# Local attention in two pieces of 1024 positions instead of three of 684, and the gate products of one pair moved back

## The chip, the cores and the metric

The kernel runs on one core of a Trainium2 chip. The core has four engines that compute and a queue of transfers. TensorE (PE) multiplies matrices and writes the results to PSUM, a small memory of eight banks. ScalarE (ACT) evaluates functions and copies. VectorE (DVE) adds and multiplies elementwise. GpSimd (POOL) does some elementwise work out of the way. SyncE (SP) issues nearly all DMA transfers. Each engine executes its own instructions in their written order, and waits on semaphores for the others.

The metric is device microseconds from one launch, the median of several runs. Lower is better.

## The reference

The input x has 2048 rows and 1024 columns. Two attention blocks read it, and a gate for each row mixes their results. Cut to what matters:

```python
g = sigmoid((x * gate_w).sum(-1, keepdims=True))
# A: linear attention, 32 heads of 32 columns
pq, pk = phi(q), phi(k)                 # phi(t) = (t + 1 if t > 0 else exp(t)) + 1e-6
kv, z  = pk^T v, pk.sum(positions)      # summed over all 2048 positions
a = (pq kv) / (pq z + 1e-6) @ A_wo
# B: each position looks back at 8 positions, 2 apart (itself, -2, ..., -14)
logits = (q . k[pos - 2*w]) * 32 ** -0.5      # w = 0..7; before position 0: masked
b = softmax(logits) v @ B_wo
out = g * a + (1 - g) * b
```

All inputs and the output are bfloat16.

## The kernel before

**Rows.** Block B only ever looks at positions of the same parity. So x is split by parity, p = 0 (even) and p = 1 (odd), with 1024 rows each, and within a parity the window is 8 consecutive rows. x is loaded transposed, in 16 tiles of 128 rows. A *pair* is two tiles 512 rows apart; pairs 0 to 3 are even rows and pairs 4 to 7 odd rows. SP issues the loads in order of pairs (`x_loads`).

**Products.** Every projection is done by `Group` with a scheme of seven products in place of eight: each of `m1` to `m7` is four matmuls of 512 columns (eight in the output stage), into a PSUM bank X or Y of the group. Between products that add onto the same bank, ScalarE copies the bank away (`save`: M1s after `m1`, U2s after `m6`, U4s after `m5`), and DVE adds a saved copy to what is in the other bank (`acc`, line 234). So `m6`, then the copy U2s, then `m5`, then the copy U4s, then `m3` are a chain on bank X. `run` writes out the order on TensorE. With g the new group and p the one before it is

```python
g.m1, g.m2, p.m3, g.m6, p.m4, g.m7, g.m5
```

so that a group is finished (`m3`, `m4`) while the next is under way. The groups are: values of B (`vb_group`, rows), keys and queries of B (`k_group`, `q_group`, columns of 4 heads by 32 for 1024 rows: slice nn and parity p), keys and values of A (`ka_group`, `va_group`), queries of A, and the output products. When an A key group finishes a row tile, it has ScalarE evaluate `exp` on it at once (`eA`, line 520).

**Side work.** After each product `side` lets one step of other work in. Generators wait in `queue`; each yields two numbers, how many products later it may go on, and how many products the shared PSUM buffer `s` (four banks, one buffer, used by attention, by kv products and by A outputs alike) counts as taken. One such generator is `attn`, queued for each of 8 combinations of nn and p two products after the queries' last product. In what follows such a combination is a round.

**Attention before.** The 1024 positions of a parity are cut into 18 blocks of 57, taken in couples j = 0 to 8, one block for each half of the partitions (b = 0, 1). Blocks hold 1026 positions, so the key and query buffers are 2050 columns wide with two zeroed columns, and the buffers V_d and OB_d in memory have SPAN = 1026 rows, of which the last two of V_d are filled with zeros. A block of 57 queries needs 64 keys: its own positions and 7 before. Columns of nn cover two chunks ch of heads. A piece t (0, 1, 2) covers 3 couples of both chunks:

- `scores(t)`: 48 matmuls of 57 columns on quarter tiles of the array (line 672), one ScalarE exp over 4 x 342 columns (678), one DVE product with the mask of zeros and ones (680).
- `pv(t)`: 48 matmuls of 57 columns with the values `vw` (690) and 8 of 342 columns that sum the weights over the keys (696); ScalarE's logarithm and exp for the reciprocal of the sums (702, 704), DVE's copy nB of the weighted values (703), DVE's product oB (706; two buffers), and a store to OB_d (707).

The order of a round is scores(0), scores(1), pv(0), scores(2), pv(1), pv(2), with at least three products between.

**Gates.** `gate(t)` is eight matmuls of one column for a tile (line 442), into one bank `gps`. `xsums(pair)` are four DVE sums of a pair's x; the last writes over half of the tile's data that the gate reads. In the beginning gates stand between groups of B values: `gates(3)` within vb_group(2), `gates(4)` behind it, `gates(5)` behind vb_group(3), `gates(6, 7)` behind vb_group(4).

Of the kernel before, what the change touches and what calls it, by code (L numbers as in the profile page):

```python
# [8 lines left out]
ACT = mybir.ActivationFunctionType  # L9
ALU = mybir.AluOpType  # L10
# [4 lines left out]
P = 128  # L15
QB = 57
NPAIR = 9
TW = 6 * QB
SPAN = 3 * TW
EPS = 1e-6  # L20
RATE_R = 0.8
OA_DELAY = 5
# [5 lines left out]
def kernel(  # L28
# [27 lines left out]

    consts = ctx.enter_context(tc.tile_pool(name="consts", bufs=1))
    dram = ctx.enter_context(tc.tile_pool(name="dram", bufs=1, space=bass.MemoryType.DRAM))
    V_d = [dram.tile([SPAN, D], BF16, name=f"V_d{p}") for p in range(2)]
    OB_d = [dram.tile([8, P, SPAN], BF16, name=f"OB_d{p}") for p in range(2)]  # L60
    OA_d = [[dram.tile([512, D], BF16, name=f"OA_d{p}{i}") for i in range(2)] for p in range(2)]

    chainp = ctx.enter_context(tc.tile_pool(name="chainp", bufs=5))
# [135 lines left out]

    maskp = consts.tile([P, 2, 6, QB], BF16, name="maskp")
    nc.gpsimd.memset(maskp[:, :, 0, :], 0.0)
    for w in range(8):
        for base in (7 - w, 71 - w):
            nc.gpsimd.affine_select(out=maskp[:, 0, 0, :], in_=maskp[:, 0, 0, :], compare_op=ALU.not_equal,
                                    fill=1.0, base=base, pattern=[[1, QB]], channel_multiplier=-1)
        nc.gpsimd.affine_select(out=maskp[0:64, 1, 0, :], in_=maskp[0:64, 1, 0, :], compare_op=ALU.not_equal,
                                fill=1.0, base=-w, pattern=[[1, QB]], channel_multiplier=-1)
    nc.gpsimd.tensor_copy(out=maskp[64:P, 1, 0, :], in_=maskp[64:P, 0, 0, :])  # L210
    for e in range(1, 6):
        nc.gpsimd.tensor_copy(out=maskp[:, 0, e, :], in_=maskp[:, 0, 0, :])
        nc.gpsimd.tensor_copy(out=maskp[:, 1, e, :], in_=maskp[:, 1 if e == 3 else 0, 0, :])
    ones = consts.tile([P, 32], BF16, name="ones")
    nc.gpsimd.memset(ones[:], 1.0)
    for p in range(2):
        nc.gpsimd.dma_start(out=V_d[p][1024:SPAN, :].rearrange("r (a e) -> (r a) e", e=P), in_=warm[0:16, 0:P])
    bd = consts.tile([P, 4, 33], F32, name="bd")
    nc.gpsimd.memset(bd[:], 0.0)
    for i in range(4):  # L220
# [125 lines left out]
    def step(force=False):  # L346
        seen = set()
        for entry in list(queue):
            if entry[4] in seen:
                continue  # L350
            seen.add(entry[4])
            if not force and (entry[0] > state["now"] or state["free"] > state["now"]):
                continue
            state["free"] = state["now"] + entry[3]
            try:
                delay, entry[3] = next(entry[1])
                entry[0] = state["now"] + delay
                state["steps"] += 1
                return True
            except StopIteration:  # L360
                queue.remove(entry)
                return step(force)
        return False
# [176 lines left out]
    def va_group(w, pair):  # L540
        vs = v_tiles("vA")

        def kv():
# [18 lines left out]
            if last:  # L562
                nc.vector.tensor_tensor(out=KVz[:].rearrange("p c (g e) -> p c g e", g=4),
                                        in0=KVacc[:, :, None, :].broadcast_to([P, 8, 4, 33]),
                                        in1=bd[:, None, :, :].broadcast_to([P, 8, 4, 33]), op=ALU.mult)
            yield 2, 2

        def done(i):
# [84 lines left out]
            f()  # L653


    def q_of(t, j, b):
        return TW * t + 2 * QB * j + QB * b

    def attn(nn, p, kT, qT, vw):

        def scores(t):
            s = side_ps("s")
            for ch in range(2):
                for j in range(3):
                    e = (3 * ch + j) * QB
                    for b in range(2):
                        q0 = q_of(t, j, b)
                        k0 = max(0, q0 - 7)  # L670
                        for g in range(4):
                            nc.tensor.matmul(s[64 * b:64 * b + 64, g, e:e + QB],  # L672
                                             lhsT=kT[32 * g:32 * g + 32, 1024 * ch + k0:1024 * ch + k0 + 64],
                                             rhs=qT[32 * g:32 * g + 32, 1024 * ch + q0:1024 * ch + q0 + QB],
                                             start=True, stop=True)
            PT = ptp.tile([P, 4, TW], BF16, name="PT", tag="PT")
            with tc.high_priority():
                nc.scalar.activation(out=PT[:], in_=s[:, :, 0:TW], func=ACT.Exp, scale=SCALE)  # L678
            m = maskp[:, 0 if t else 1, :, :].rearrange("p i q -> p (i q)")
            nc.vector.tensor_tensor(out=PT[:], in0=PT[:], in1=m[:, None, :].broadcast_to([P, 4, TW]), op=ALU.mult)  # L680
            return PT

        def pv(t, PT):
            o = side_ps("o")
            for e in range(6):
                ch, j = divmod(e, 3)
                for g in range(4):
                    for b in range(2):
                        rows = slice(64 * b, 64 * b + 64)
                        nc.tensor.matmul(o[32 * g:32 * g + 32, 2 * b, QB * e:QB * e + QB],  # L690
                                         lhsT=vw[rows, 3 * t + j, 4 * ch + g, :],
                                         rhs=PT[rows, g, QB * e:QB * e + QB], start=True, stop=True)
            for g in range(4):
                for b in range(2):
                    rows = slice(64 * b, 64 * b + 64)
                    nc.tensor.matmul(o[32 * g:32 * g + 32, 2 * b + 1, 0:TW], lhsT=ones[rows, :], rhs=PT[rows, g, :],
                                     start=True, stop=True)
            nB = ofp.tile([P, 2, TW], F32, name="nB", tag="nB", bufs=1)
            rB = ofp.tile([P, 2, TW], F32, name="rB", tag="rB", bufs=1)
            oB = ofp.tile([P, 6, 2, QB], BF16, name="oB", tag="oB", bufs=2)  # L700
            with tc.high_priority():
                nc.scalar.activation(out=rB[:], in_=o[:, 1:4:2, 0:TW], func=ACT.Ln)  # L702
                nc.vector.tensor_copy(out=nB[:], in_=o[:, 0:4:2, 0:TW])  # L703
            nc.scalar.activation(out=rB[:], in_=rB[:], func=ACT.Exp, scale=-1.0)
            num, r = (ap.rearrange("p b (e q) -> p e b q", e=6) for ap in (nB[:], rB[:]))
            nc.vector.tensor_tensor(out=oB[:], in0=num, in1=r, op=ALU.mult)
            nc.sync.dma_start(out=OB_d[p][2 * nn:2 * nn + 2, :, TW * t:TW * t + TW].rearrange("c p q -> p c q"),
                              in_=oB[:].rearrange("p (c j) b q -> p c (j b q)", c=2))

        last = None  # L710
        yield 0, 2
        for t in range(4):
            if t < 3:
                PT = scores(t)
                yield (1, 3) if last else (3, 3)
            if last:
                pv(*last)
                yield 1, 3
            last = (t, PT)

    def load_v(nn, p):
        vw = vwp.tile([P, NPAIR, 8, 32], BF16, name="vw", tag="vw")
        for b, j, n in ((0, 0, 1), (0, 1, 8), (1, 0, 9)):
            k0 = max(0, q_of(0, j, b) - 7)
            src = cols_of(V_d[p][k0:k0 + 64, :], nn)
            src = bass.AP(src.tensor, src.offset, [src.ap[0], [2 * QB * D, n], src.ap[-1]])
            nc.sync.dma_start(out=vw[64 * b:64 * b + 64, j:j + n, :, :].rearrange("p n h e -> p n (h e)"), in_=src)
        return vw
# [1 line left out]
    its = {}  # L730

    def k_group(w, nn, p):
        kT = kqp.tile([P, 2050], BF16, name="kT", tag="kq")
        nc.gpsimd.memset(kT[:, 2048:2050], 0.0)
        its[nn, p] = kT
        return Group(col_ops(w, p), lambda i, j, ps, add: acc(kT[:, 1024 * j + 512 * i:1024 * j + 512 * i + 512], ps, add))

    def q_group(w, nn, p):
        qT = kqp.tile([P, 2050], BF16, name="qT", tag="kq")
        nc.gpsimd.memset(qT[:, 2048:2050], 0.0)  # L740
        vw = load_v(nn, p)

        def done(i):
            if i == 1:
                add_side(2, attn(nn, p, its[nn, p], qT, vw), p, "attn")
        return Group(col_ops(w, p), lambda i, j, ps, add: acc(qT[:, 1024 * j + 512 * i:1024 * j + 512 * i + 512], ps, add), done)


    Wo = {}
# [117 lines left out]
    defer(2, xsums(3) + xsums(0))  # L867
    run(lambda: vb_group(2), 0)
    x_loads(6, 7)
    gates(4)  # L870
    defer(1, xsums(4) + xsums(1))
    run(lambda: vb_group(3), 0)
    load_k(0, 13)()
    load_q(0, 20)()
    gates(5)
    defer(2, xsums(5))
    run(lambda: vb_group(4), 0)
    gates(6, 7)
# [101 lines left out]
```

## Time and profile before

| | |
|---|---|
| runs | 463.18, 463.40, 464.05 us; median 463.4 us |
| profiled execution | 462.85 us, of which the span of instructions is 461.1 us |
| TensorE | 450.9 us busy (98%), 5137 matmuls |
| ScalarE | 241.6 us busy (52%) |
| DVE | 286.1 us busy (62%) |
| GpSimd | 56.6 us busy (12%) |
| DMA | 51.65 MB, 112 GB/s over the span |
| score matmuls (line 672) | 1152 of 57 columns, 66.8 to 287.2 us |
| value matmuls (lines 690, 696) | 1152 of 57 and 192 of 342 columns, 73.2 to 298.8 us |

A timeline line gives the start, the length, the engine, the line of the kernel, the operation, what it writes and reads, and the shape. A line with x4 merges four instructions in a row. Matmuls are pipelined: the length of one (379 ns at 512 columns) is longer than the distance to the next, so the distance of starts is the cost. A bracket at the end of a line names the idle time before it and what ended it.

### The profile page before, as it was taken

How to read it: one execution, taken by the hardware profiler on the slowest of the kernel's cores; microseconds unless marked ns; L12 is line 12 of the kernel's file. 1: busy time of each engine (PE TensorE's matmuls, PEld its weight loads, DVE VectorE, ACT ScalarE, POOL GpSimd, SP SyncE). 2: the span in 40 equal slices, each digit the busy share in tenths (PEclk: the TensorE clock that was granted, in tenths of full speed). 3: DMA queues.
4: the chain of work that ended last, by engine and by line, in shares of the span. 5: the costliest groups of instructions: out<-in, count | busy, mean ns of one | idle time of the engine just before them, and what ended most of it. 6: DMA issues, size and time to landing. Idle time of an engine off the chain costs nothing. (4 is left out here: it accounts for less than half of the span.)

```text
span 461.1 us, 11964 instructions
## 1 busy us (share of the span) xinstructions
PE 450.9 (98%) x5137; PEld 217.7 (47%) x5137; DVE 286.1 (62%) x458; ACT 241.6 (52%) x367; POOL 56.6 (12%) x130
## 2 busy tenths in 40 slices
PE   8989999999999999999999999999999999999997
PEld 5445444444444444444444444445554444444444
DVE  0547668769848577486684856579876973164312
ACT  1233447568568386584855848536676545222221
POOL 8000000000000000000000000006676313000000
PEclk9999999999999999999999999999999999999999
DMA  8999811590211702106021066464239872699211
GB/s 180 187 221 246 275 41 64 147 256 19 57 28 33 157 21 64 22 20 159 18 71 28 17 146 181 112 188 103 68 77 205 177 171 81 118 189 174 68 47 46
DMA packets 117941, 51.65 MB, mean 112 GB/s; under 512 B 77696, under 2 KB 115840, under 8 KB 117888
## 3 DMA queue, kind: packets, MB, share of 16 engines
q1 hardware_dynamic: 117520, 50.62, 47.1%
q8 instruction: 40, 0.66, 0.6%
q10 hardware_dynamic: 272, 0.26, 0.2%
q0 software_dynamic: 96, 0.01, 0.1%
q14 instruction: 13, 0.11, 0.1%
HBM read 25.69 MB, written 16.79 MB: 92 GB/s over the span
## 5 line engine op out<-in xcount | busy, mean ns | idle before, releaser
L252 PEld LDWEIGHTS <-xT 128*128 128x128 bf16 (+1 forms) x352 | 32.6, 98 | 37.6 <-issue 0.6
L252 PE MATMUL X<-T,SS 128*128 128x512 f16 x176 | 45.2, 379 | 0.0
L635 PE MATMUL Q<-xT,WS 128*128 128x512 bf16 x192 | 43.9, 379 | 0.5 <-DVE vA L234 0.5
L261 ACT COPY U4s<-X 128x512 f32<-128x512 f32 x40 | 23.2, 581 | 37.3 <-PE X L252 37.2
L252 PEld LDWEIGHTS <-WS 128*128 128x128 bf16 (+1 forms) x288 | 27.1, 98 | 32.9 <-issue 2.5
L678 ACT ACTIVATE PT<-s 128x1368 bf16<-128x1368 f32 x24 | 31.5, 1314 | 19.9 <-PE s L672 19.9
L252 PE MATMUL Y<-W,xT 128*128 128x512 bf16 (+1 forms) x152 | 39.1, 380 | 0.0
L252 PEld LDWEIGHTS <-SS 128*128 128x128 f16 x264 | 24.4, 98 | 27.8
L252 PE MATMUL Y<-xT,WS 128*128 128x512 bf16 (+1 forms) x144 | 37.0, 379 | 0.2 <-DVE qT L234 0.2
L252 PE MATMUL X<-SS,TS 128*128 128x512 f16 x144 | 36.9, 379 | 0.1
L680 DVE TENSOR_TENSOR PT<-PT,maskp 128x1368 bf16<-128x1368 bf16 x24 | 20.8, 867 | 20.8 <-ACT PT L678 20.8
L252 PEld LDWEIGHTS <-TS 128*128 128x128 f16 x216 | 20.5, 98 | 25.2 <-issue 1.8
L261 ACT COPY M1s<-X 128x512 f32<-128x512 f32 x40 | 23.3, 583 | 11.8 <-PE X L252 11.7
L261 ACT COPY U2s<-X 128x512 f32<-128x512 f32 x40 | 23.3, 582 | 10.4 <-PE X L252 10.4
L635 PEld LDWEIGHTS <-WS 128*128 128x128 bf16 x192 | 18.2, 98 | 20.6 <-issue 0.8
L252 PEld LDWEIGHTS <-oT 128*128 128x128 bf16 (+1 forms) x176 | 17.1, 98 | 21.8 <-DMA oT<-OA_d 1.5
L703 DVE COPY nB<-o 128x684 f32<-128x684 f32 x24 | 20.8, 867 | 6.3 <-ACT rB L702 6.0
L603 POOL TENSOR_TENSOR obA<-ofv,rec 128x512 bf16<-128x512 f32 x22 | 24.0, 1109 | 0.9
L640 ACT ACTIVATE eq<-Q 128x512 bf16<-128x512 f32 x24 | 14.3, 598 | 18.4 <-PE Q L635 17.3
L252 PE MATMUL X<-T,oS 128*128 128x512 f16 x96 | 22.7, 379 | 0.0
L252 PE MATMUL X<-W,SS 128*128 128x512 bf16 x88 | 22.7, 380 | 0.0
L252 PE MATMUL X<-W,xT 128*128 128x512 bf16 x88 | 22.6, 380 | 0.0
(137 smaller groups left out, 759.6 us busy)
## 6 DMA issues: line engine op xcount, KB each, us to landing
OB_d<-oB SPq DMA_DIRECT2D x24, 171.0 KB, 2.9
V_d<-va SPq DMA_DIRECT2D x16, 256.0 KB, 3.0
WS<-in_B_wqkv_dram SPq DMA_DIRECT2D x16, 256.0 KB, 4.2
W<-in_A_wqkv_dram SPq DMA_DIRECT2D x8, 512.0 KB, 7.0
OA_d<-obA SPq DMA_DIRECT2D x16, 256.0 KB, 2.4
out_dram<-osb SPq DMA_DIRECT2D x30, 128.0 KB, 2.0
oT<-OB_d SPq DMA_DIRECT2D x12, 256.0 KB, 4.8
vw<-V_d SPq DMA_DIRECT2D x8, 288.0 KB, 4.7
```

Of the source, the lines that this page charges most:

```text
L252: nc.tensor.matmul(ps[:], lhsT=lhsT, rhs=rhs, start=start and kc == 0, stop=kc == self.nk - 1, skip_group_check=True)
L261: nc.scalar.copy(out=s[:], in_=ps[:])
L603: nc.gpsimd.tensor_tensor(out=ob[:, k:k + 2], in0=of[:, k:k + 2, :, 0:32], in1=rec[:, k:k + 2].broadcast_to([P, 2, 8, 32]), op=ALU.mult)
L635: nc.tensor.matmul(ps[:], lhsT=w.W[:, kc, j * P:j * P + P], rhs=xT[p][:, kc, i, :], start=kc == 0, stop=kc == 7, skip_group_check=True)
L640: nc.scalar.activation(out=es[i][:, j, :], in_=ps[:], func=ACT.Exp)
L678: nc.scalar.activation(out=PT[:], in_=s[:, :, 0:TW], func=ACT.Exp, scale=SCALE)
L680: nc.vector.tensor_tensor(out=PT[:], in0=PT[:], in1=m[:, None, :].broadcast_to([P, 4, TW]), op=ALU.mult)
L703: nc.vector.tensor_copy(out=nB[:], in_=o[:, 0:4:2, 0:TW])
```

## The change

- The pieces of attention become the two chunks of heads. A piece covers 1024 positions of one chunk: 72 score matmuls, an exp and a mask product over 4 x 512 columns, 72 value matmuls and 8 sums of 512 columns, and chains of 1024 columns behind them. The order of a round is scores(0), scores(1), pv(0), pv(1). Score pieces are set at least four products apart, value pieces three.
- The last couple of blocks has 56 positions instead of 57, so that 16 x 57 + 2 x 56 = 1024 positions fit exactly. The zeroed columns and the memsets for them go; the zero rows of V_d and their two DMAs go. The last block reads 64 keys that begin at 960, and the mask is built anew for a width of 512 (32 selections instead of 24).
- oB has one buffer of 1024 columns instead of two of 684, is written by two DVE products (the couples of 57 and the last), and one store per chunk goes to contiguous rows of 2 KB.
- The values are loaded by four DMAs instead of three for a round.
- A outputs (kind "oa") are taken from the queue only when KVz is written.
- `gates(4)` moves behind vb_group(3), next to `gates(5)`.

```diff
-        def scores(t):
+        def scores(ch):
             s = side_ps("s")
...
+            for j in range(NPAIR):
+                for b in range(2):
+                    q0, n, k0 = block(j, b)
+                    for g in range(4):
+                        nc.tensor.matmul(s[64 * b:64 * b + 64, g, QB * j:QB * j + n],
+                                         lhsT=kT[32 * g:32 * g + 32, ch, k0:k0 + 64],
+                                         rhs=qT[32 * g:32 * g + 32, ch, q0:q0 + n], start=True, stop=True)
+            PT = ptp.tile([P, 4, 512], BF16, name="PT", tag="PT")
             with tc.high_priority():
-                nc.scalar.activation(out=PT[:], in_=s[:, :, 0:TW], func=ACT.Exp, scale=SCALE)
...
+                nc.scalar.activation(out=PT[:], in_=s[:], func=ACT.Exp, scale=SCALE)
+            nc.vector.tensor_tensor(out=PT[:], in0=PT[:], in1=maskp[:, None, :].broadcast_to([P, 4, 512]), op=ALU.mult)
...
-            oB = ofp.tile([P, 6, 2, QB], BF16, name="oB", tag="oB", bufs=2)
+            oB = ofp.tile([P, 1024], BF16, name="oB", tag="oB", bufs=1)
...
-        for t in range(4):
-            if t < 3:
-                PT = scores(t)
-                yield (1, 3) if last else (3, 3)
-            if last:
-                pv(*last)
-                yield 1, 3
-            last = (t, PT)
+        yield 0, 4
+        PT = [scores(0)]
+        yield 1, 4
+        PT.append(scores(1))
+        for ch in range(2):
+            yield 1, 3
+            pv(ch, PT[ch])
+        yield 1, 3
...
-    gates(4)
     defer(1, xsums(4) + xsums(1))
     run(lambda: vb_group(3), 0)
     load_k(0, 13)()
     load_q(0, 20)()
-    gates(5)
+    gates(4, 5)
```

## The prediction

> **What bounds the kernel now.** I read the page first: its busy times, then the waits and the timeline of TensorE, then the queues of ScalarE (ACT) and VectorE (DVE) in one attention round. The page:
>
> ```profile
> PE 450.9 (98%) x5137; PEld 217.7 (47%) x5137; DVE 286.1 (62%) x458; ACT 241.6 (52%) x367; POOL 56.6 (12%) x130
> ...
> PEclk9999999999999999999999999999999999999999
> ```
>
> TensorE has matmuls in flight 98% of the span, at an undiminished clock. So an edit is worth what it does to TensorE's issue: matmuls taken out, or stops of TensorE taken out or put in. Busy time hides short stops (a matmul of 512 columns is shown as 379 ns and issues every 216), so I take starts from the timeline. One attention round, TensorE:
>
> ```profile
> 191.88 1.03 PE L252 MATMUL Y<-xT,WS 128*128 128x512 bf16 x4
> 192.84 0.57 PE L672 MATMUL s<-qT,kT 32*64 32x57 bf16 x48
> 193.34 1.04 PE L252 MATMUL X<-W,SS 128*128 128x512 bf16 x4
> 194.21 1.03 PE L252 MATMUL X<-SS,TS 128*128 128x512 f16 x4
> 195.07 1.03 PE L252 MATMUL Y<-T,xT 128*128 128x512 f16 x4
> 196.03 0.55 PE L690 MATMUL o<-PT,vw 64*32 64x57 bf16 x48
> 196.39 0.37 PE L696 MATMUL o<-PT,ones 64*32 64x342 bf16 x8
> 196.69 1.04 PE L252 MATMUL Y<-xT,WS 128*128 128x512 f16 x4
> 197.57 1.03 PE L252 MATMUL X<-SS,TS 128*128 128x512 f16 x4
> 198.43 1.03 PE L252 MATMUL X<-W,xT 128*128 128x512 bf16 x4
> 199.50 0.56 PE L672 MATMUL s<-qT,kT 32*64 32x57 bf16 x48
> ```
>
> Here a product of four matmuls takes 0.864 us from start to start. A score piece (s) set between two adds 193.34-191.88-0.864 = 0.596; a value piece (o) adds 196.69-195.07-0.864 = 0.756. The last line starts 0.11 late (198.43+0.96 = 199.39): a wait for the DVE copy nB. There are eight rounds of three score and three value pieces.
>
> The one early stop, and ScalarE in the same round:
>
> ```profile
> 27.00 1.03 PE L252 MATMUL X<-T,SS 128*128 128x512 f16 x4
> 28.45 0.35 PE L442 MATMUL gps<-gw,xT 128*128 128x1 bf16 x8 [0.43 <-DMA xT<-in_A_x_dram]
> 29.91 0.35 PE L442 MATMUL gps<-gw,xT 128*128 128x1 bf16 x8 [1.11 <-DMA xT<-in_A_x_dram]
> 30.12 1.02 PE L252 MATMUL X<-W,xT 128*128 128x512 bf16 x4
> ```
>
> ```profile
> 193.47 1.31 ACT L678 ACTIVATE PT<-s 128x1368 bf16<-128x1368 f32 x1 [0.81 <-PE s L672]
> 194.68 0.58 ACT L232 CAST tA<-X 128x512 bf16<-128x512 f32 x1
> 195.29 1.06 ACT L520 ACTIVATE eA<-tA 128x1024 bf16<-128x1024 bf16 x1
> 196.25 0.57 ACT L261 COPY U2s<-X 128x512 f32<-128x512 f32 x1
> ```
>
> The copy U2s takes bank X away after its sixth product (m6, at 194.21); the fifth (m5, at 197.57) adds onto the same bank and waits for that copy. It ends at 196.82, 0.75 us before m5.
>
> **The change, part by part.**
>
> 1. *The gates of pair 4.* From 27.00 to 30.12 are 3.12 us; the product itself is 0.86, sixteen gate matmuls 0.40 (22.74 to 23.14 elsewhere in that timeline). So 1.86 us are wait. Moved one group back, both pairs' gates stand near 33.9, and the last x tile of pair 5 landed at 32.65 (issued by SP at 28.37). Nothing is late there: the 0.8 us of the 32 gates is the old work, and pair 4's in-place DVE difference, which overwrites what the gate reads, comes in the queue only after the next group's first product. **-1.86** (if pair 5 came 1.3 us later, the gain would begin to shrink).
>
> 2. *Pieces.* Matmul count and columns hardly change: 144 score and 144 value matmuls a round before and after; the sums over keys are 24x342 columns before and 16x512 after. What goes is entering and leaving. A score piece of 48 has 47 starts in about 0.57-0.21 = 0.36 us, 7.7 ns each; the other 0.23 of 0.596 is fixed. Of a value piece, 48 starts take 0.35 (196.03 to 196.39 rounded), 7.4 ns each. After: score 0.596+24x0.0077 = 0.78; value 0.756+24x0.0074+170 columns x 0.42 ns (0.864/4/512) = 1.005. Old: 24x(0.596+0.756) = 32.4. New: 16x1.785 = 28.6. **-3.85.** The Trainium skill, TensorEngine Tiling (Array Packing), Key Properties, says that changing the tiling mode drains TensorE. It states no price; counted by matmuls and columns alone this part would be 0, by the row's fixed share it is 3.85. I take the row.
>
> 3. *Waits of the third pieces.* The 0.11 above occurs in six rounds, and in the second round are 0.63 (same copy, behind a large weight sum on DVE) and 0.05. There is no third piece any more: **-1.4.** The eighth round's last value piece, now among the A queries at 298.43, is pulled forward, and with it goes a late vA addition: Q starts at 302.35 instead of 299.97+1.73, **-0.65.**
>
> 4. *The new wait.* The first score piece now needs both halves of qT, so the last DVE addition of that group. In all eight rounds that addition ends 0.07 us before the piece starts (188.88+0.69 against 189.64). Handing over costs about 0.05, as where nB (ends 199.45) releases the piece at 199.50. Cost 0, by 0.02; bound 0 to 0.1 each.
>    The second score piece is put four products after the first, not three, since the first exp is longer. So it now comes *after* the group's third product (m3), and ScalarE's built order becomes tA cast, eA exp, the long exp of scores, then U2s. Count from the start of m3. TensorE reaches m5 after m3 with the turn into tiling (0.86+0.09), the score piece (0.55+0.14), m6, m4 and m7 (2.59): 4.23. ScalarE: m3 ends at 0.65+0.38 = 1.03; cast 0.04+0.58; eA 0.03+1.06, to 2.74; then the exp of 2048 columns. Rows: 684 columns 0.74 (a logarithm), 1368 columns 1.31, so 0.85 ns a column and 1.89 for 2048, overlapping its predecessor by 0.1 (194.68 starts before 193.47+1.31): 4.53; U2s 0.57-0.1: 5.02; handover 0.05. m5 can start at 5.07, **0.84 late**, where it had 0.75 to spare. This occurs where a group of A keys is being finished in front: seven of eight rounds, since the first has no eA. **+5.9** (bounds 0.6 and 1.0 a round).
>    Behind the blocked m5 stands the value piece, behind U2s the second eA exp, the U4s copy and the logarithm of the sums; they shift with it and are not paid twice.
>    The rule that speaks against this change is in the Trainium skill, TensorE: Matmul & The Clock Gate, the table at its head: ScalarE's queue is strictly first in, first out. The row agrees in kind: X was ready at 195.24, the U2s copy began at 196.25 behind eA. Were it free to pass, this term would be 0 and the sum -7.5. I take the queue.
>
> 5. *Second value piece.* It needs the o buffer free: the logarithm (1.03 by the same slope) and DVE's nB of 1024 columns (rows: 0.69 at 512, 0.87 at 684, so 1.23). On DVE ahead of nB stand the second mask product (0.42 at 512, 0.87 at 1368, so 1.23) and about 2.4 us: kT's addition and key functions or weight sums. Following that queue, nB ends about level with the piece's turn: 0 to 0.04 in ordinary rounds, about 0.5 in the second, with its 1.2 us weight sums. **+0.7**, bounds 0 and 2.4 (0.3 a round); the lower since only the second round has long sums.
>
> 6. *oB, now one buffer.* The second piece's quotient waits for the first store. The store is issued some 2.9 us before DVE would write again; DVE's next addition (vA) is not needed until 0.9 later. Landing takes:
>
> ```profile
> OB_d<-oB SPq DMA_DIRECT2D x24, 171.0 KB, 2.9
> V_d<-va SPq DMA_DIRECT2D x16, 256.0 KB, 3.0
> ```
>
>    The new store is 256 KB in rows of 2 KB, like V_d's: 3.0. Cost 0 by about 0.85 us.
>
> 7. *Rest.* At the end TensorE stops 1.16 for the transposed OA tiles (350.64 against 348.62+0.86) and 0.49 at 339.17. The A outputs now come four matmuls (0.86) earlier beside the queries, ScalarE serves a query exp ahead of each (+0.3 on the POOL-and-DMA chain): **-0.5**, bounds -1.2 and +0.3. The longer mask building on POOL (32 selections instead of 24), done by about 15 us, has until 68; the fourth vw load adds about 0.5 us of SP and value pieces come 9 us after it; the removed zero fills and memsets were waited for by nobody on the path. All 0.
>
> Sum: -1.86-3.85-1.4-0.65+5.9+0.7-0.5 = **-1.7** against the profiled execution's 462.85 (span 461.1 and 1.8 around it). The runs' median is 0.55 above that; I carry the difference over: **461.8 us.**
>
> **Rivals.**
> *A. The exp does not block (5 in 100).* If the second exp ran early enough or m5's wait had slack, the sum is -7.5: 455.9. For it: ACT is busy only 52%. Against: the walk above, in which every duration is a row.
> *B. The store of oB decides (15 in 100), slower.* Landing was 2.1 to 4.1 for OB_d and up to 7.8 for V_d in the busy start. Beyond 3.85 us from issue, each excess stops DVE's vA addition, and with it the fourth product of that group on TensorE. At an average of 4.5 in eight rounds: +5.2, so 467.0. It turns the result slower from about 4.2 on. Against: during attention the DMA engines are only 32% busy.
> *C. The terms cancel (17 in 100).* Block at its upper bound (+1.1), second value pieces at 0.1 a round: 463.3, not to be told from before.
> *D. The forecast (63 in 100)*: 461.8, own range 460.2 to 462.6.
>
> **How the numbers follow.** Below 0.2% (0.9 us) this kernel's measurement cannot tell a difference, so faster is below 462.5. Faster: D but for a few in 100, and A, 0.65. Same: C, 0.17. Slower: B and the tail of C, 0.18. The range takes D with its bounds and C, leaves out A and the far half of B: 459.8 to 464.3.
>
> **What would show it.** Gate matmuls near 34 with no DMA wait; score pieces about 0.78 and value pieces about 1.0; a wait of m5 on the U2s copy of 0.8 us seven times, with U2s directly behind the exp of 2048 columns; no wait longer than 0.1 at a first score piece; a DVE wait on the oB store under 0.9 us. The prediction is wrong if m5 does not wait (A), or a fourth product waits on DVE after each second value piece (B).

## The result, and the profile after

The changed kernel takes 461.28 us (median of 4, 461.04 to 461.71), the kernel before 463.29 beside it (462.98 to 464.05): ratio 0.9955, 95% interval 0.9938 to 0.9972. The profiled execution took 461.23 with a span of 459.5, against 462.85 and 461.1. TensorE's last matmul starts at 455.37 instead of 457.35. So 1.98 us have gone from TensorE's row of starts, and that row is what has to be explained.

The page of the changed kernel. TensorE has 64 matmuls fewer, and the rows of OB_d move in less time (last column: median us from issue to landing). The loads of before come first; its stores, shown in the prediction, took 2.9:

```profile
oT<-OB_d SPq DMA_DIRECT2D x12, 256.0 KB, 4.8
```

```profile
PE 447.7 (97%) x5073; PEld 217.7 (47%) x5073; DVE 282.3 (61%) x450; ACT 235.9 (51%) x343; POOL 59.4 (13%) x117
...
OB_d<-oB SPq DMA_DIRECT2D x16, 256.0 KB, 2.1
oT<-OB_d SPq DMA_DIRECT2D x12, 256.0 KB, 4.0
```

What TensorE waits for (total us, times, longest), first before, then after:

```profile
PE gps L442 <- DMA xT<-in_A_x_dram: 1.5, 2, 1.1
...
PE X L252 <- DMA oT<-OA_d: 1.0, 1, 1.0
...
PE s L672 <- DVE nB L703: 0.6, 1, 0.6
PE Q L635 <- DVE vA L234: 0.5, 1, 0.5
PE oA L592 <- ACT ofv L594: 0.3, 1, 0.3
PE Y L252 <- DVE qT L234: 0.2, 1, 0.2
```

```profile
PE X L252 <- ACT U2s L261: 4.5, 7, 0.7
...
PE o L689 <- DVE nB L701: 0.6, 1, 0.6
PE o L689 <- issue: 0.5, 1, 0.5
```

The six waits shown of the first list are gone: for pair 4's x tiles, the OA tiles, nB (ahead of a third score piece), vA, ofv and qT. At the head of the second stands a new one: a product into bank X that waits for the copy U2s, seven times. TensorE's timeline shows the places:

```profile
33.31 1.03 PE L252 MATMUL X<-T,SS 128*128 128x512 f16 x4
34.17 0.94 PE L444 MATMUL gps<-gw,xT 128*128 128x1 bf16 x32
34.97 1.02 PE L252 MATMUL X<-W,xT 128*128 128x512 bf16 x4
...
161.76 1.03 PE L252 MATMUL X<-W,SS 128*128 128x512 bf16 x4
162.72 0.77 PE L673 MATMUL s<-qT,kT 32*64 32x57 bf16 x72
163.42 1.04 PE L252 MATMUL X<-SS,TS 128*128 128x512 f16 x4
...
166.84 1.02 PE L252 MATMUL X<-SS,TS 128*128 128x512 f16 x4 [0.66 <-ACT U2s L261]
...
289.17 0.65 PE L689 MATMUL o<-PT,vw 64*32 64x57 bf16 x61
290.32 0.23 PE L689 MATMUL o<-PT,vw 64*32 64x57 bf16 x11 [0.51 <-issue]
...
347.60 1.03 PE L252 MATMUL X<-SS,TS 128*128 128x512 f16 x4
348.66 1.90 PE L252 MATMUL X<-W,oT 128*128 128x512 bf16 x8
```

The 32 gate matmuls follow their product after 0.86 us, with no wait. In the round, m3 starts at 161.76 and m5 at 166.84: 5.08 us, where the prediction counted 5.07. ScalarE in the same stretch:

```profile
162.88 0.59 ACT L232 CAST tA<-X 128x512 bf16<-128x512 f32 x1 [0.74 <-PE X L252]
163.50 1.06 ACT L522 ACTIVATE eA<-tA 128x1024 bf16<-128x1024 bf16 x1
164.46 1.86 ACT L678 ACTIVATE PT<-s 128x2048 bf16<-128x2048 f32 x1
166.22 0.58 ACT L261 COPY U2s<-X 128x512 f32<-128x512 f32 x1
```

U2s, which m5 needs, stands behind the key exp and the exp of 2048 columns. Bank X had been ready since 164.46 (m6's start at 163.42 and 1.04), and the copy began at 166.22. At 289 one value piece is cut into 61 and 11 matmuls by a stop that no semaphore explains; nothing in the prediction spoke of it.

At the end, TensorE goes from its last product of A queries to the first output product. Before, this cost 2.02 us from start to start; in the changed kernel, by the last two lines above, 1.06:

```profile
348.62 1.03 PE L252 MATMUL X<-SS,TS 128*128 128x512 f16 x4
350.64 1.68 PE L252 MATMUL X<-W,oT 128*128 128x512 bf16 x7 [0.99 <-DMA oT<-OA_d]
```

Taken from start to start in the two traces:

| step | forecast, us | measured, us |
|---|---|---|
| gates of pair 4 | -1.86 | -1.86 |
| entering and leaving 16 fewer pieces | -3.85 | -3.36 |
| waits at third pieces | -1.4 | -1.38 |
| late vA ahead of Q | -0.65 | -0.65 |
| two waits in round 2 (0.38 for qT, 0.23 for bank X) gone | not foreseen | -0.6 |
| m5 behind U2s | +5.9 | +5.69 |
| second value piece, waiting for nB | +0.7 | +0.86 |
| stop inside the last value piece | not foreseen | +0.65 |
| A outputs (0.48 to 0) and first output product (1.16 to 0.20) | -0.5 | -1.44 |
| first score piece; one oB buffer | 0 | 0 |
| start of the program (first product of a group at 23.41 instead of 23.14) | 0 | +0.27 |
| many differences of at most some hundredths | 0 | -0.16 |
| sum | -1.7 | -1.98 |

The start is scatter: in the thirteen profiled executions of this case the first product of a group starts at 23.13 to 23.58, whatever the edit. The rows from the fewer pieces to the stop in the last value piece come to +1.2. So the bigger pieces by themselves make TensorE's row longer, and the end, which gains 1.44, pays for them.

### The profile page after: what moved, and what is told of

The parts are those of the page before. It is cut to its first block, busy times and chain, and to the rows that moved or that the text cites. A ratio compares the mean times of both kernels' runs of the same rounds, so it can differ in the third digit from the quotient of the medians.

```text
span 459.5 us, 11765 instructions
## 1 busy us (share of the span) xinstructions
PE 447.7 (97%) x5073; PEld 217.7 (47%) x5073; DVE 282.3 (61%) x450; ACT 235.9 (51%) x343; POOL 59.4 (13%) x117
## 4 chain that ended last, share of the span: by engine, by line
PE 90%; ACT 6%; DMA 1%; SPq 1%; issue 0%; DVE 0%; ACTq 0%; DVEq 0%
PE X L252 41%; PE Y L252 28%; PE Q L638 9%; PE K L497 3%; ACT PT L678 3%; PE o L689 2%; ACT eA L522 2%; PE oA L595 2%; DMA xT<-in_A_x_dram 1%; PE s L673 1%; PE kps L556 1%; ACT tA L232 1%; PE o L694 1%; PE Y L287 1%; ACT U2s L261 1%; PE gps L444 1%
## 5 line engine op out<-in xcount | busy, mean ns | idle before, releaser
L252 PEld LDWEIGHTS <-WS 128*128 128x128 bf16 (+1 forms) x288 | 28.1, 98 | 33.6
L463 POOL MEMSET vA<- 128x32 bf16 x16 | 3.9, 249 | 269.9 <-DVE eA L525 145.0
L678 ACT ACTIVATE PT<-s 128x2048 bf16<-128x2048 f32 x16 | 29.9, 1869 | 15.1 <-PE s L673 15.0
L679 DVE TENSOR_TENSOR PT<-PT,maskp 128x2048 bf16<-128x2048 bf16 x16 | 19.6, 1224 | 22.1 <-ACT PT L678 22.1
L606 POOL TENSOR_TENSOR obA<-ofv,rec 128x512 bf16<-128x512 f32 x22 | 25.7, 1187 | 0.9
L701 DVE COPY nB<-o 128x1024 f32<-128x1024 f32 x16 | 19.5, 1220 | 6.0 <-ACT rB L700 6.0
L700 ACT ACTIVATE rB<-o 128x1024 f32<-128x1024 f32 x16 | 16.4, 1025 | 12.2 <-DVE oB L707 9.4
```

The source lines that it names most:

```text
L252: nc.tensor.matmul(ps[:], lhsT=lhsT, rhs=rhs, start=start and kc == 0, stop=kc == self.nk - 1, skip_group_check=True)
L606: nc.gpsimd.tensor_tensor(out=ob[:, k:k + 2], in0=of[:, k:k + 2, :, 0:32], in1=rec[:, k:k + 2].broadcast_to([P, 2, 8, 32]), op=ALU.mult)
L678: nc.scalar.activation(out=PT[:], in_=s[:], func=ACT.Exp, scale=SCALE)
L679: nc.vector.tensor_tensor(out=PT[:], in0=PT[:], in1=maskp[:, None, :].broadcast_to([P, 4, 512]), op=ALU.mult)
L700: nc.scalar.activation(out=rB[:], in_=o[:, 1:4:2, :], func=ACT.Ln)
L701: nc.vector.tensor_copy(out=nB[:], in_=o[:, 0:4:2, :])
```

## The experiments

The theory: the gate move gives its 1.8 us and nothing takes its place; the rest of the change comes to about nothing. Rival views: the gates' stop would have been made good later anyway; m5 is late for another reason than the key exp; the end moved because of the order of the A outputs, not because of the rows of OB_d. Each edit is made to the changed kernel unless the text says "before". Ratios are to the kernel before on the same chip in the same session. What the last section tells of the clock makes some spreads wide; "full clock" below means a mean granted clock above 0.997.

**1. The gates back in their old place.**

```
     x_loads(6, 7)
+    gates(4)
     defer(1, xsums(4) + xsums(1))
...
-    gates(4, 5)
+    gates(5)
```

> The changed kernel with the gates of pair 4 put back ahead of the group of B values, everything else as changed. Theory: the early stop of TensorE for the x tiles of pair 4 returns whole, 1.8 us (590 + 1244 ns in the trace of before), so about 463.1 us against 461.3 of the changed kernel, and level with before (463.3, ratio 0.999). Rival: the gates only hid a later DMA wait or late x sums; then the stop returns but a later one shrinks, and the time stays within 0.5 us of the changed kernel.

Measured: 463.71 us (462.37 to 465.83), ratio 0.9993 (0.9975 to 1.0012). TensorE's timeline, and its window from 30 to 34 us (columns: length, busy us of PE, PEld, DVE, ACT and POOL, granted clock, DMA share, GB/s):

```profile
27.96 0.34 PE L444 MATMUL gps<-gw,xT 128*128 128x1 bf16 x8
30.18 0.35 PE L444 MATMUL gps<-gw,xT 128*128 128x1 bf16 x8 [1.88 <-DMA xT<-in_A_x_dram]
...
31.63 1.91 PE L252 MATMUL Y<-W,xT 128*128 128x512 bf16 x4
```

```profile
30.00:34.00 4.00, 3.82 (x18) 1.54 (x19) 0.51 (x2) 0.58 (x1) 0.00 (x0) 0.61 1.02 198
```

The wait is back in one piece of 1.88, and in this execution it cost more than itself: the product after it takes 1.91 instead of 1.03, at a granted clock of 0.61. The seven waits on U2s stay at 4.5 us. With the gates in the old place, the interval doesn't tell the rest of the change from nothing; among executions at full clock the difference to before is 0.5 us (462.92 against 463.41).

**2. Before, with the gates alone moved.**

```
     x_loads(6, 7)
-    gates(4)
     defer(1, xsums(4) + xsums(1))
...
-    gates(5)
+    gates(4, 5)
```

> The kernel before with the gates of pair 4 moved behind the next group, and nothing else. Theory: 1.8 us of DMA wait go and nothing takes their place; about 461.5 us against 463.3, ratio 0.996. That would be nearly the whole measured gain of the change, with the pieces of attention worth about nothing net. Rival: later work in the kernel before absorbs it (x sums of pairs 6 and 7 late), and the gain is below 0.5 us.

Measured: 461.14 us (460.64 to 461.36), ratio 0.9930 (0.9909 to 0.9952). The wait of the gates is gone, the waits of the third pieces and of the OA tiles are about as before:

```profile
PE X L252 <- DMA oT<-OA_d: 0.8, 1, 0.8
PE s L672 <- DVE nB L703: 0.6, 1, 0.6
```

At full clock the gain is 2.3 us (461.14 against 463.48), of which the wait explains 1.9. This one moved line gives about the whole gain of the change; runs 1 and 2 agree that everything else together, the pieces and the shorter rows of OB_d, comes to about nothing.

**3. The key exp behind U2s.** The function that finishes a tile of A keys issues its exp two places later, and after the last copy of the kind that U2s is. All is computed as before.

```
+    last_save = [None]
...
-                nc.scalar.copy(out=s[:], in_=ps[:])
+                last_save[0] = nc.scalar.copy(out=s[:], in_=ps[:]).ins
...
-            defer(0, phi(e[:], ts[i][:]))
+            def keys():
+                with tc.issue_after(last_save[0]):
+                    ops = phi(e[:], ts[i][:])
+                defer(0, ops)
+            later(2, keys)
```

> The changed kernel, but ScalarE's exp of an A key tile is bound to come after the U2s copy of the group in flight, so U2s stands directly behind the long exp of scores. Theory: ScalarE's first-in-first-out queue is the whole reason that m5 waits 0.77 to 0.83 us in seven rounds; with eA out of the way U2s ends about 0.1 us before m5's turn, the seven waits go (5.7 us), and the time is about 455.6 us, ratio to before 0.983. Rival: m5 is only the first of two waits; DVE (key functions and nB later by a microsecond) stops the second value piece instead by up to 0.6 us a round, and the time is 458 to 460 us.

Measured: 458.74 us (457.94 to 460.36), ratio 0.9884 (0.9862 to 0.9907). ScalarE and TensorE in the next round, and what TensorE waits for:

```profile
190.76 0.59 ACT L233 CAST tA<-X 128x512 bf16<-128x512 f32 x1 [0.74 <-PE X L253]
191.43 1.88 ACT L683 ACTIVATE PT<-s 128x2048 bf16<-128x2048 f32 x1
193.21 0.58 ACT L262 COPY U2s<-X 128x512 f32<-128x512 f32 x1
193.67 2.02 ACT L523 ACTIVATE eA<-tA 128x1024 bf16<-128x1024 bf16 x2
```

```profile
193.90 1.03 PE L253 MATMUL X<-SS,TS 128*128 128x512 f16 x4
...
198.91 0.74 PE L694 MATMUL o<-PT,vw 64*32 64x57 bf16 x72 [0.36 <-DVE nB L706]
...
287.90 0.23 PE L694 MATMUL o<-PT,vw 64*32 64x57 bf16 x11 [1.52 <-issue]
288.41 1.89 PE L253 MATMUL X<-T,SS 128*128 128x512 f16 x4
```

```profile
PE o L694 <- DVE nB L706: 2.9, 7, 1.0
```

U2s now ends before m5's turn, and all seven waits on it are gone: the order on ScalarE was the cause. But the expected 455.6 is not reached, because of what is late next. The second value piece waits for nB in seven rounds, 3.35 us from start to start against 0.86 in the changed kernel, as the other view had it. The stop inside the last value piece is longer too, and in this execution the product after it took 1.89 instead of 1.03.

**4. The same edit to the kernel before**, where m5 had 0.75 us to spare:

> The kernel before with ScalarE's exp of A key tiles bound behind the U2s copy, as was worth 3 to 6 us in the changed kernel. Theory: in the kernel before m5 has 0.75 us to spare, so there is nothing to win; within 0.5 us of before, and up to 0.3 us a round worse where key functions on DVE now come later and delay nB. Rival: ScalarE's order costs the kernel before as well, in waits that its profile puts elsewhere; then 1 us or more faster.

Measured: 464.06 us (462.75 to 464.78), ratio 0.9980 (0.9963 to 0.9997). TensorE waits at the same places as before. By the ratio it is 0.9 us faster, a little more than the 0.5 us expected; where these come from isn't shown, and at full clock it is 0.4 (463.03 against 463.46, three executions each). The 3 us of run 3, with the longer score exp in front of U2s, aren't there.

**5. The second score piece one product sooner.**

```
-        yield 0, 4
+        yield 0, 3
         PT = [scores(0)]
```

> The changed kernel, but the second score piece is set three products after the first instead of four, as in the kernel before; so it stands ahead of m3, and ScalarE's built order becomes exp, exp, tA, U2s, eA. Theory: the seven waits of m5 go, since the exp is done with 0.9 us earlier against the products; the first exp of 1.87 us still frees the buffer about 0.7 us before the second score piece. About 456 us, ratio 0.984. Rival: the score buffer is not free after three products and the piece waits about 0.3 us in each of eight rounds, or U4s and the logarithm, now later on ScalarE, stop m3 and the value pieces: 458 to 460 us.

Measured: 462.89 us (462.27 to 464.78), ratio 0.9972 (0.9954 to 0.9991). This expectation missed by 7 us.

```profile
PE o L689 <- issue: 2.2, 1, 2.2
PE Y L252 <- DVE kT L234: 1.8, 3, 0.7
...
PE X L252 <- ACT U2s L261: 1.4, 5, 0.3
```

The key exp does stand behind the long score exp now, and the old wait of m5 is gone. In its place are waits on VectorE's additions (kT), a shorter one on a U2s copy at another place, and a longer stop in the last value piece. Moving the piece by one product took one wait away and made others, of about the same sum.

**6. OB_d in rows that are no multiple of 256 bytes.** The changed kernel's rows hold 1024 elements of 2 bytes, 2048; those of before held 1026, 2052. Here the changed kernel gets the old row length and uses 1024 of each row:

```
-    OB_d = [dram.tile([8, P, 1024], BF16, ...
+    OB_d = [dram.tile([8, P, 1026], BF16, ...
...
-   nc.sync.dma_start(out=OB_d[p][2 * nn + ch, :, :], in_=oB[:])
+   nc.sync.dma_start(out=OB_d[p][2 * nn + ch, :, 0:1024], in_=oB[:])
```

> The changed kernel with the rows of OB_d 1026 elements apart again (2052 B), of which 1024 are used; nothing else changes, so all pieces of 256 B that the output stage loads start at odd places again as in the kernel before. Theory: the rows of 2048 B are why OB_d loads land in 4.0 us instead of 4.8, and why TensorE's stop ahead of the first output product fell from 1.16 to 0.20 us; here it returns to 0.8 to 1.2 us, and the time is 0.6 to 1.0 us above the changed kernel, about 462.1 us. Rival: the stop fell because A outputs come earlier beside the queries; then loads are slower but the stop stays near 0.2 to 0.5 us and the time within 0.3 us of 461.3.

Measured: 463.27 us (462.38 to 464.82), ratio 0.9971 (0.9957 to 0.9985). Its transfers, and TensorE at the first output product with its window:

```profile
OB_d<-oB SPq DMA_DIRECT2D x16, 256.0 KB, 2.9
oT<-OB_d SPq DMA_DIRECT2D x12, 256.0 KB, 5.0
```

```profile
347.31 1.03 PE L252 MATMUL X<-SS,TS 128*128 128x512 f16 x4
...
350.39 3.58 PE L252 MATMUL X<-W,oT 128*128 128x512 bf16 x8 [2.06 <-DMA oT<-OA_d]
```

```profile
350.00:354.00 4.00, 3.61 (x12) 1.42 (x13) 2.07 (x3) 0.00 (x0) 0.73 (x1) 0.57 1.04 244
```

The same bytes in the same number of transfers take 5.0 us instead of 4.0 to load and 2.9 instead of 2.1 to store. The OA tiles that TensorE waits for are loaded in the same queue, and it stops 2.2 us instead of 0.20 (350.39 - 347.31 - 0.864), then runs at a clock of 0.57. The stop is twice as long as expected, and so the time is 1.2 us above the 462.1 expected. With the old rows the changed kernel at full clock is 0.25 us below before (463.16 against 463.41), though the gates' wait is gone. A stop that is 1.0 longer than the 1.16 of before is part of that, the pieces are the rest.

**7. Before, with rows of 1152 elements (2304 bytes, nine times 256).**

```
-    OB_d = [dram.tile([8, P, SPAN], BF16, ...
+    OB_d = [dram.tile([8, P, 1152], BF16, ...
```

> The kernel before with the rows of OB_d 1152 elements apart (2304 B) in place of 1026 (2052 B), so that pieces of 256 B read by the output stage start at multiples of 256 B; nothing else. Theory: its loads land about 0.8 us sooner, the transposes behind them are issued sooner, and TensorE's stop ahead of the first output product falls from 1.16 us to about 0.3; 0.8 us less, ratio 0.998. Rival: the stop is set by the A outputs on GpSimd; the loads land sooner and the time stays, ratio 1.000.

Measured: 462.34 us (461.78 to 464.1), ratio 0.9965 (0.9944 to 0.9985).

```profile
OB_d<-oB SPq DMA_DIRECT2D x24, 171.0 KB, 2.6
oT<-OB_d SPq DMA_DIRECT2D x12, 256.0 KB, 4.1
```

The loads take 4.1 us instead of the 4.8 of before, and the stop of 1.16 ahead of the first output product is under 0.05 (it starts at 350.20, 0.87 after the product before it). The pieces here are the old ones: so the shorter stop at the end comes from the row's length, not from the pieces' order. The first transposed load of OA, behind these loads in the queue, lands 6.18 us (before) and 6.79 (run 6) after its issue with rows of 2052 bytes, and 4.76 (changed kernel) and 4.28 (run 7) with rows of 2048 and 2304. The Trainium skill (DMA: Bandwidth & Descriptors, How a descriptor splits into AXI transactions) says that a read which doesn't start on a 256-byte boundary begins at the boundary below, and that the bytes in front are fetched for nothing. Both runs agree with that in kind; how many transactions there were isn't in the traces.

**8. The output weights of A loaded later.** The stop in the last value piece comes while four loads of 512 KB (Wo of A) are landing. Here they are asked for twelve places later:

```
-    rows += [(ka[7], lambda: load_wo("A", A_wo), lambda: defer(24, Wo["A"].sums(), 3)), ...
+    rows += [(ka[7], lambda: later(12, lambda: (load_wo("A", A_wo), defer(12, Wo["A"].sums(), 3)))), ...
```

> The changed kernel with the four loads of A_wo (512 KB each) issued twelve products later, after the eighth attention round, and their sums due at the same product as before. Theory: TensorE's stop inside the last value piece (0.65 us in the profile of the changed kernel, 0.55 to 2.35 us in its variants, always ahead of the same TensorE instruction, 1.25 to 1.6 us after a 16 KB packet of the instruction queue has landed) comes from that packet standing behind these loads; it goes, and so does any half-speed stretch that follows it, so about 460.6 us, ratio 0.994 or a little less. Rival: the stop belongs to the density of instructions at that place (a score and two value pieces of 160 instructions close together), and stays between 0.5 and 2.4 us; ratio 0.9955.

Measured: 460.43 us (460.2 to 460.79), ratio 0.9912 (0.9881 to 0.9943). The stop is gone, the waits on U2s are as in the changed kernel. The other view, that the stop belongs to the crowd of small matmuls at that place, fell. For the size, it was run again directly beside the changed kernel:

> The changed kernel again, so that its variants of this call are compared on one chip. It should show seven m5 waits of 0.77 to 0.83 us as before, and a stop in the last value piece of 0.5 to 2.4 us; ratio to before 0.993 to 0.997.

> The changed kernel with the four A_wo loads issued twelve products later. Theory (packets of TensorE's own instructions wait behind those loads): no stop in the last value piece, 0.5 to 2 us below the changed kernel of the same call. Rival (the absence in one profile was chance): a stop of 0.5 us or more at the same instruction, and no difference between the two.

Measured: the changed kernel 460.91 us (460.7 to 462.64), ratio 0.9915 (0.9887 to 0.9943); with later weights 460.34 (460.11 to 460.59), 0.9906 (0.9877 to 0.9935). The two sets of runs don't touch; 0.57 lies between the medians. The last value piece of the one, then of the other:

```profile
291.46 0.23 PE L689 MATMUL o<-PT,vw 64*32 64x57 bf16 x11 [1.48 <-issue]
```

```profile
288.89 0.74 PE L689 MATMUL o<-PT,vw 64*32 64x57 bf16 x72
```

**9. Both edits together**, the key exp behind U2s (its DVE functions put four places later, so that nB comes sooner) and the later weights: run 3's diff with `defer(4, ops)` and run 8's.

> The changed kernel with ScalarE's exp of A key tiles bound behind the U2s copy, DVE's key functions moved four products later so that they stand behind nB, and the A_wo loads twelve products later. Theory: the seven m5 waits (5.7 us), the seven waits of the second value piece that took their place (3.4 us of those returned) and the stop in the last value piece all go; 7 us less than the changed kernel, about 454.5 us, ratio 0.981. Rival: the key functions, pushed back, hold their buffers and stop the kv products or the A key groups instead; 456 to 458 us.

Measured: 456.03 us (455.8 to 456.33), ratio 0.9819 (0.9790 to 0.9848). TensorE's first wait:

```profile
PE o L694 <- DVE nB L706: 1.7, 3, 1.4
```

Of seven waits for nB three are left, 1.42 in round 2 and twice 0.26. The expected 454.5 isn't reached, and the time is in the range of the other view, but none of the waits that it named is in the list. This is the fastest of all, 5.3 us below the changed kernel's 461.28 and 7.4 below before (463.48 for the executions beside it at full clock). It is also 5.1 below run 2, which has the gates' move and the old pieces. The rows' length (1.4 us by run 7 at full clock, 462.11 against 463.48) and the later key exp in the kernel before (0.9 by run 4) are less than half of that. So the bigger pieces do pay, once what they make late is moved out of the way.

## Why the prediction was right, and where its terms were off

The forecast was 461.8 us and a gain of 1.7; measured are 461.28 and 2.0. The steps that carry the change, the gates and the blocked m5, were right in place, cause and size; that the sum came within 0.3 is in part luck, as some other terms missed both ways. By its own steps:

1. *Gates:* right, -1.86 both, and run 2 shows that the gain reaches the end. The prediction named two reasons why nothing would be late next (the x tiles have landed, the DVE difference comes later), and nothing was.
2. *Pieces:* the mechanism held (fixed cost of entering and leaving), the size was 0.5 too large. From start to start less the product, a score piece takes 0.792 and a value piece 1.026, for 0.78 and 1.005; 16 x 1.818 - 24 x 1.352 is -3.36. (The prediction's own figures give -3.89, not -3.85.) The marginal price of a small matmul was put at 7.7 and 7.4 ns from rounded rows; from starts it is 8.3 ns both times ((561 - 361.5)/24 and (615.5 - 416)/24), and 16 pieces of each kind carry the difference.
3. *Third pieces and vA:* right, -1.38 and -0.65. Missed were two waits of round 2, for DVE's qT and behind ScalarE's bank copy, that left with the third piece: another -0.6.
4. *m5 behind U2s:* right in place, count and size. Seven waits of 774 to 829 ns instead of 840, sum 5.69 for 5.9. The walk along ScalarE's queue gave 5.07 from m3 to m5, the trace 5.08; its items are off by up to 0.06 (the long exp starts 2.70 after m3 for 2.64, U2s ends at 5.04 for 5.02), and added up exactly they give 5.05. Run 3 shows the cause, since with the key exp behind U2s all seven vanish.
5. *Second value piece:* +0.86 for +0.7, with 0.65 of it in round 2, 0.11 in round 8 and 0.04 in each of three others. That it was a cover used up to the edge is shown by run 3: as soon as m5 was on time, nB was late seven times.
6. *oB:* no cost to TensorE. Landing took 2.1 us and not 3.0, at most 3.5, below the 3.85 from which rival B counted. The row chosen as nearest (V_d's store) was too high.
7. *Rest:* put at -0.5 with a bound of -1.2, measured -1.44. The oA wait left as foreseen (0.48). What was mis-sized is the stop ahead of the first output product: the text moved it by the order of the A outputs, but its transfers also became quicker by the row's length, from 4.8 to 4.0 us a load. Runs 6 and 7 show this from both sides. The text listed the new row length only for the store.

The stop in the last value piece, +0.65, was not foreseen, and no line of the profile of before pointed to it. The misses of -0.6 (round 2) and -0.9 (end) stand against +0.5 (pieces), +0.65 (the stop) and +0.27 (the start): the sum was closer than its terms.

Rival A (no block) fell with the seven waits, B with the landing times. C, the terms cancelling, is what happens to everything but the gates, as runs 1 and 2 show; for the whole change the gates remain on top.

## What to carry to other kernels

When a longer instruction is put on an in-order queue, follow the queue item by item to the next instruction that the bounding engine needs: that walk gave the new wait within some hundredths of a us, and it named the edit that took it away. Then walk on to the next wait before promising the gain: of the 5.7 us that moving the key exp freed, 2.5 came back as waits on another engine. And take a buffer's row length in memory as a cost of its own; 2 extra elements in a row of 1024 were worth 1.4 us (run 7, at full clock) to 2 us (run 6), mostly at the one place that waits for those transfers.

## What the runs showed of the hardware

**A stop at one place of TensorE's code.** The stop in the last value piece always comes ahead of the same instruction, the 4063rd matmul of the program, in all five traces of runs that have it whole. In four of these it is the 62nd of the 72 matmuls of its piece; in run 5, where the pieces stand elsewhere, it is the 66th. So the stop belongs to a place in TensorE's code and not to the piece. On a queue of their own, of the kind "instruction", come packets of 16 KB: 40 before for 10274 matmuls and weight loads of TensorE, 39 in the changed kernel for 10146, about one for every 260. That they are TensorE's code is read from this count. Ahead of each stop one of them comes in while the Wo loads are landing, and TensorE goes on 1.25 to 1.54 us after it has come:

| run | last Wo load lands | packet moves | TensorE goes on |
|---|---|---|---|
| changed kernel | 288.64 | 287.94 to 289.07 | 290.32 |
| changed kernel, again beside run 8 | 289.67 | 288.95 to 290.01 | 291.46 |
| gates back | 292.79 | 292.18 to 293.27 | 294.60 |
| key exp later | 286.44 | 285.34 to 286.40 | 287.90 |
| second score piece sooner | 291.27 | 288.41 to 289.49 | 291.01 |
| OB_d rows of 1026 | 289.15 | 287.47 to 288.49 | 290.03 |
| weights later (first run) | after 303 | 286.43 to 287.76 | no stop |

The stop was 0.55 to 2.35 us long. Runs 8 and 9, with later loads, have none: that the loads cause it is shown by that. That the packet queues behind them is argued from the times; in run 5 it came 1.8 us before the last load.

**A stop can cost the clock as well.** After the gate stop of run 1, the stop of run 3 and that of run 6, about eight matmuls of 512 columns were issued every 426 ns instead of 216, for about 3.4 us, which added 1.6 to 1.7 us. (The windows of 4 us above, with 0.57 and 0.61, take in more than that stretch.) The clock records of these traces have 0.5 for 3.41 us each time, after 23.89, 283.31 and 344.75 us at full clock. Those are 7, 83 and 101 times 3.413, so the clock changes on a grid of 3.413 us.

Counted back, each of the three stops (1.88, 1.52 and 2.06 us idle) lies whole in the cell of the grid just before the slow one. In run 5's profiled execution an edge of the grid, at 290.56, falls into the stop of 2.35 that ended at 291.01, and the clock stayed. The Trainium skill (TensorE: Matmul & The Clock Gate, Part 1) tells of a free-running window of about 3.4 us, after an idle one of which the clock is halved. The length agrees, and a grid that doesn't keep step with the kernel fits a loss that comes in some executions and not in others. But here windows with only 1.5 to 2.1 us of idle time were followed by the half clock. How much is enough isn't settled: in run 5 the part of the stop ahead of the edge was 1.8 us, and nothing followed.

It shows in the executions without a trace too. Of 66 of the kernel before in the three sessions of experiments, 37 have a mean granted clock of 0.993 to 0.997 and 29 one above; in the first of these sessions the medians are 465.12 and 463.41, 1.7 apart. Without the gate stop, the executions of run 2, of the changed kernel beside run 8 and of runs 8 and 9, 29 in all, have the full clock. Runs 3, 5 and 6, without the gate stop but with long stops of another kind, have 2 of 6, 3 of 10 and 1 of 12 below. At full clock run 1's median is 462.92 and below it 464.60, against 461.28 of the changed kernel: so the gates' place is worth 1.6 us where the clock holds and 3.3 where it doesn't. This is why the changed kernel's ratio was 0.9915 beside run 8, where 11 of 14 executions of before were below, and 0.9955 in the first comparison, where no run of before was above 464.05. The forecast knew nothing of it, and its gain of 1.7 is to be held against executions at full clock.
